# Dynamic convolution with gated projection on one core: softmax loads and stores as single transfers, x loaded by batch from POOL's queue

## The chip, the cores and the metric

The kernel runs on one core of a Trainium2 chip. The metric is the device time of one execution in microseconds. The programs of this case are timed in several runs, and the median counts; one more execution is taken with the hardware profiler, and all rows of the profile come from it.

## What is computed

Two steps on x of shape (8, 4224, 192), in float32. First a dynamic convolution: for each position and each of 8 heads, seven weights go through a softmax and mix the last seven rows of x. Then a gated layer on the result: a causal convolution of five taps per channel gives a gate through a sigmoid, a projection gives a value, and gate times value is projected again.

```python
# attention-like part: B=8, S=4224, D=192, H=8 heads of 24 channels, K=7
w = exp(weight_gen - max(weight_gen, -1)); w = w / (sum(w, -1) + 1e-09)
x_pad = concat(zeros(B, K-1, D), x)                    # causal
a[b,s,h,g] = sum_k w[b,s,h,k] * x_pad[b, s+k, h*24+g]
# gated part, on a
gate_pre[b,s,d] = sum_{k<5} conv_w[k,d] * a_pad[b, s+k, d]
out = (sigmoid(gate_pre) * (a @ w_val)) @ w_out
```

## The kernel before

**Groups.** The sequence is cut into 36 groups of 118 positions (the last has 94), each for all 8 batches. For a group, 128 rows of x (118 and what the convolutions reach back) lie in SBUF as `xt`, partition by row, batch and channel along the free side; three such buffers rotate. The softmax weights of the group lie in `tb` as a banded matrix per batch and head, so that the dynamic convolution becomes matmuls of 128 x 32 by 128 x 122 on TensorE (PE): `bank` (line 432), 128 of them per group in four kinds, one for each pair of half-filled output tiles. Two `tb` buffers rotate.

The row order inside the partitions is special: partition 8 * i + j holds row 16 * j + i of the group. So a chunk j of 16 successive rows sits on every eighth partition, and one transfer fills one chunk for all batches: `load_x` (line 410) and `load_t` (line 419), eight of each per group.

**After the banks.** ScalarE (ACT) copies the results out of PSUM into `A`, `B` and `S` (`evac`, lines 443 to 450). Some heads land apart from the others, in `S`, and eight small transfers per group on POOL's queue (`move`, lines 459 and 461) put them into holes of `A` and `B`. Then the gate's first tap on ACT (line 473), four more on VectorE (DVE, line 478), the sigmoid on ACT (483), the values matmul on PE (`val`, lines 492 to 499), gate times value on DVE (506, 508), the last projection on PE (`omm`, 519 and 526), a copy on ACT (541) and two stores on SP's queue (550).

**Softmax.** It runs ahead of the groups in ten parts. A part of R rows per partition covers 16 R positions of each batch: 128 partitions, partition 8 * q + b for stretch q of batch b. `load` (272) brings the part's weights with a few more rows into `wt`, one transfer per batch, eight in all. Reductions, subtraction, exponential, reciprocal and product follow on DVE and ACT (lines 282 to 307). `spread` (319, ACT) writes the weights, with gaps, into `zt`, twelve rows of a part at a time, and `store` (325) puts these into the DRAM scratch `zd`, again one transfer per batch. `load_t` reads `zd` back as a band. The parts have 8, 8, 16, six times 34, and 28 rows; a part has one to three `zt` pieces, 25 in all.

**The order.** No scheduler sorts the instructions. A planner (`Order`) takes each operation with its engine, an estimated duration, a key and its dependences, plays them through, and issues each engine's instructions in the order so found. The order is fixed in the program: on each engine, and on each engine's DMA queue, an instruction that waits holds up all behind it. The durations given with `add` decide the order, not the time taken on the chip. The queue of a transfer is the engine that issues it: in the program before, SP issues all x and tb loads, all output stores, nearly all softmax loads and a few z stores; POOL issues the moves and most z stores; ACT issues four loads and four stores of the first part.

Of the kernel before, what the change touches and what calls it, by code (L numbers as in the profile page):

```python
# [89 lines left out]
def tile_dynconv_gated_moe(  # L90
# [9 lines left out]
    nc = tc.nc  # L100

    B, S, D = x.shape
    H, K = wg.shape[2], wg.shape[3]
    C = D // H
    KC = conv_w.shape[0]
    P = 128
    HD = P // 2
    Q = 32
    PAD = K - 1
    HALO = KC - 1  # L110
    FRONT = PAD + HALO
# [12 lines left out]
    G = 16  # L124
# [121 lines left out]
    class Softmax:  # L246
# [17 lines left out]

        def load(self, b, eng):
            R, n = self.R, self.n
            flat = self.wt.rearrange("p r h k -> p (r h k)")
            off = wg.offset + (b * S + self.r0) * ROW

            def part(q, c0, c1):  # L270
                src = bass.AP(tensor=wg.tensor, offset=off + c0 * ROW, ap=[[R * ROW, q], [1, (c1 - c0) * ROW]])
                eng.dma_start(out=flat[b:b + B * q - B + 1:B, c0 * ROW:c1 * ROW], in_=src)  # L272

            if b == B - 1 and self.r0 + HP * R == S:
                part(HP, 0, R)
                part(HP - 1, R, n)
            else:
                part(HP, 0, n)

# [40 lines left out]

        def store(self, c, z, b, eng):
            a, e = self.zc[c]
            d0 = zd[b, 1 + self.r0 + a, :]
            dst = bass.AP(tensor=d0.tensor, offset=d0.offset, ap=[[self.R * PITCH, HP], [1, (e - a) * PITCH]])
            eng.dma_start(out=dst, in_=z[b:P:B, 0:e - a].rearrange("p r c -> p (r c)"))  # L325

# [3 lines left out]
    def softmax(r0, R, k0, k1, early, k2, behind=()):  # L330
# [3 lines left out]
        n = s.n * ROW  # L334
        ld = []
        b0 = add("DVE", 0.06, early - 1e-3, s.begin, old, behind=behind)
        for n_, b in enumerate((0, 4, 1, 5, 2, 6, 3, 7)):
            q = QUEUES[n_ % 2] if r0 == 0 else QUEUES[0]
            ld.append(add(q[0], 0.45, early + 1e-3 * n_, lambda b=b, e=q[1]: s.load(b, e), [b0],
                          bytes=HP * n * 4))  # L340
        h = len(s.cut)
# [19 lines left out]
        for c, (a, b) in enumerate(s.zc):  # L361
            z = zt[len(zstore) % 2]
            old = zstore[-2] if len(zstore) > 1 else zinit[len(zstore)]
            need = [nm for nm, (c0, c1) in zip(norms, s.cut) if c0 < b + PAD and c1 > a]
            kk, cp = key(), []
            for e in range(2):
                for o in range(2):
                    cp.append(add("ACT", act((b - a) // 2 * (NPR - o) * H), kk,
                                  lambda c=c, z=z, e=e, o=o: s.spread(c, z, e, o), [*need, *old]))
            sts = []  # L370
            for n_, i in enumerate((0, 4, 1, 5, 2, 6, 3, 7)):
                q = QUEUES[n_ % 2 if r0 == 0 else 0 if len(soft) == 2 else 2]
                sts.append(add(q[0], 0.55, k2, lambda c=c, z=z, i=i, e=q[1]: s.store(c, z, i, e), cp,
                               bytes=HP * (b - a) * PITCH * 4))
            zstore.append(sts)
            last += cp
            rows.append((r0, sts))
# [7 lines left out]
    class Group:  # L385
# [13 lines left out]
        def rows(self, j):  # L399
# [4 lines left out]
            return lo, hi, slice(NGR * lo + j, NGR * (hi - 1) + j + 1, NGR)  # L404

        def load_x(self, j):
            lo, hi, p = self.rows(j)
            src = bass.AP(tensor=x.tensor, offset=x.offset + (self.s - FRONT + G * j + lo) * D,
                          ap=[[D, hi - lo], [S * D, B], [1, D]])
            nc.sync.dma_start(out=self.xb[p, :, 0:D], in_=src)  # L410

# [51 lines left out]
        def part(self, g, j):  # L463

            return (self.B if g else self.A).rearrange("p (b w) -> p b w", w=self.w)[:, :, j:j + self.n]
# [158 lines left out]
    for m, gp in enumerate(gr):  # L624
        if 2 <= m < len(PARTS) - 1:
# [6 lines left out]
        late = (() if m == 0 else T[m - 1]["loadt"]) if m < 3 else ()  # L632
        d["loadx"] = [add("SP", 0.42, (-90, -35, -1)[m] if m < 3 else m - 1.9, lambda gp=gp, j=j: gp.load_x(j), old, bytes=G * B * D * 4, behind=late) for j in gp.chunks]
        use = [o for a, sts in rows if a < gp.s + n for o in sts] + [front]
        old = dep(m - 2, "bank") if m >= 2 else cleared[m % 2]
        d["loadt"] = [add("SP", 0.45, m - 1.8 + 0.01 * j, lambda gp=gp, j=j: gp.load_t(j), [*use, *old],
                          bytes=G * B * RUN * 4) for j in gp.chunks]
# [8 lines left out]
        for q, kind in enumerate((3, 2, 0, 1)):  # L646
# [10 lines left out]
            else:  # L657
# [3 lines left out]
        d["bank"], d["ev"] = list(bank.values()), ev  # L661
        mvB = [add("POOL", 0.6, m + 0.1, lambda gp=gp, k=k, u=u: gp.move(k, u), [*ev[3], *ev[2]], bytes=(Q - C) * HB * w * 4)
               for k in (4, 5) for u in range(2)]
        mvA = [add("POOL", 0.6, m + 0.2, lambda gp=gp, k=k: gp.move(k, 0), [*ev[3], *ev[0], *ev[1]], bytes=(Q - C) * HB * w * 8)
               for k in range(4)]
# [21 lines left out]
        for k in range(2):  # L687
# [3 lines left out]
        d["out"], d["oev"] = o, evs  # L691
        d["store"] = [add("SP", 0.45, m + 2.0, lambda gp=gp, i=i: gp.store(i), evs, delay=4.0,
                          bytes=n * D * 4 * (B if i == 0 else 1)) for i in range(2)]
# [27 lines left out]
```

## Time and profile before

| what | value |
|---|---|
| median of 3 runs | 625.44 us (622.83 to 625.74) |
| the profiled execution's own time | 621.07 us |
| its span, first to last instruction | 619.3 us |
| mean granted TensorE clock | 0.909 |
| busy PE, DVE, ACT, POOL | 490.9, 438.0, 342.3, 259.7 us |
| moved by the DMA engines | 123.20 MB in 135989 packets, mean 199 GB/s |
| x loads, tb loads, SP | 287 and 287 issues |
| softmax loads | 77 issues on SP, 4 on ACT |
| z stores | 176 issues on POOL, 20 on SP, 4 on ACT |
| moves | 288 issues on POOL |

How to read the rows: `L410` is line 410 of the kernel; an engine's name with a q (SPq) is its queue, where DMA issues stand with the time that the issue took, not the transfer. `out<-in` are the program's tile names. In a row of busy time, the number after the comma is the mean of one in ns. A bracket at the end of a row gives the idle time of the engine before it, and what ended it. A granted clock under 1 means that TensorE ran slower in that stretch. Busy PE includes matmuls that wait in its pipeline.

### The profile page before, as it was taken

The numbers are of one execution on the slowest core, as the hardware profiler recorded it, in microseconds if no ns is written. First come the engines' busy times: TensorE is split into PE (matmuls) and PEld (weight loads), VectorE is DVE, ScalarE is ACT, GpSimd is POOL, SyncE is SP. The second block draws the span as 40 slices with busy tenths as digits, with TensorE's granted clock in tenths as the row PEclk, the third lists the DMA queues.
The fourth block names the chain that finished last, engine by engine and source line by source line (L and its number), as shares of the span: only waits on it lengthen the run. The fifth ranks groups of instructions, "written<-read, shape, count | busy, mean of one in ns | idle before, by whom it ended". The sixth has DMA issues, their size and how long they took to land.

```text
span 619.3 us, 16002 instructions
## 1 busy us (share of the span) xinstructions
PE 490.9 (79%) x6278; PEld 335.0 (54%) x6278; DVE 438.0 (71%) x488; ACT 342.3 (55%) x531; POOL 259.7 (42%) x496
## 2 busy tenths in 40 slices
PE   2015289576999598888999997488996899999995
PEld 1012266364658365556666765366665567667753
DVE  5376559676894845987798782987885476867680
ACT  4334365567657434485667854368654546555641
POOL 9155266047434812135550764027634614322220
PEclk7557899979899889997999999589997899999999
DMA  4665579869895976767896799668878777677332
GB/s 121 158 199 156 143 218 283 235 172 270 234 270 150 263 206 169 205 180 193 226 286 180 208 264 253 203 177 245 240 194 255 200 192 183 188 195 192 84 85 85
DMA packets 135989, 123.20 MB, mean 199 GB/s; under 512 B 21866, under 2 KB 130022, under 8 KB 133226
## 3 DMA queue, kind: packets, MB, share of 16 engines
q1 hardware_dynamic: 120026, 90.83, 53.0%
q0 software_dynamic: 15632, 30.76, 17.9%
q8 instruction: 50, 0.82, 0.5%
q10 hardware_dynamic: 256, 0.58, 0.3%
q14 instruction: 25, 0.20, 0.1%
HBM read 64.55 MB, written 51.43 MB: 187 GB/s over the span
## 4 chain that ended last, share of the span: by engine, by line
PE 54%; SPq 24%; DMA 9%; ACT 5%; issue 3%; DVE 2%; POOL 2%; ACTq 0%; DVEq 0%
PE pa L432 16%; PE po L519 13%; SPq L419 10%; PE po L526 7%; SPq L410 7%; PE v L496 7%; SPq L272 5%; PE v L499 4%; PE v L494 4%; PE v L492 4%; DMA tb<-zd 3%; DMA xt<-in_x_dram 2%; DMA zd<-zt 2%; SPq L550 2%; ACT ot L541 1%
## 5 line engine op out<-in xcount | busy, mean ns | idle before, releaser
L432 PE MATMUL pa<-tb,xt 128*32 128x122 f32 (+1 forms) x4608 | 150.7, 290 | 88.4 <-DMA tb<-zd 63.5
L432 PEld LDWEIGHTS pa<-tb,xt 128*32 128x32 f32 x4608 | 138.8, 117 | 104.3 <-issue 88.6
L478 DVE SCALAR_TENSOR_TENSOR aA<-A,wf,aA 128x944 f32<-128x944 f32 (+1 forms) x144 | 171.6, 1191 | 18.6 <-ACT aA L473 13.4
L461 POOL DMA_DIRECT2D B<-S x144 | 74.1, 521 | 250.2 <-ACT B L446 240.8
L478 DVE SCALAR_TENSOR_TENSOR aB<-B,wf,aB 128x472 f32<-128x472 f32 (+1 forms) x144 | 101.2, 703 | 40.1 <-ACT aB L473 30.1
L519 PE MATMUL po<-wf,aA 128*118 128x192 f32 (+1 forms) x576 | 114.9, 344 | 11.4 <-ACT ot L541 6.2
L541 ACT COPY ot<-po 118x768 f32<-118x768 f32 (+1 forms) x72 | 57.7, 802 | 113.2 <-PE po L526 72.5
L519 PEld LDWEIGHTS po<-wf,aA 128*118 128x118 f32 (+1 forms) x576 | 92.6, 185 | 40.6 <-issue 13.8
L325 POOL DMA_DIRECT2D zd<-zt x176 | 85.0, 489 | 49.2 <-ACT zt L319 29.5
L459 POOL DMA_DIRECT2D A<-S x144 | 73.7, 519 | 29.2 <-ACT A L443 22.5
L526 PE MATMUL po<-wf,aB 64*118 64x192 f32 (+1 forms) x576 | 67.3, 352 | 14.7 <-DVE aB L508 10.2
L506 DVE TENSOR_TENSOR aA<-v,aA 128x944 f32<-128x944 f32 (+1 forms) x36 | 40.8, 1135 | 47.4 <-ACT aA L483 34.2
L450 ACT COPY S<-pa 64x488 f32<-64x488 f32 (+1 forms) x72 | 40.4, 561 | 52.1 <-PE pa L432 51.6
L496 PE MATMUL v<-A,wva 128*128 128x472 f32 (+1 forms) x144 | 63.1, 559 | 0.0
L526 PEld LDWEIGHTS po<-wf,aB 64*118 64x118 f32 (+1 forms) x576 | 45.1, 180 | 31.8 <-issue 12.9
L483 ACT ACTIVATE aA<-aA 128x944 f32<-128x944 f32 (+1 forms) x36 | 35.7, 991 | 30.5 <-DVE aA L478 30.5
L443 ACT COPY A<-pa 128x488 f32<-128x488 f32 (+1 forms) x72 | 40.6, 563 | 11.8 <-PE pa L432 10.9
L496 PEld LDWEIGHTS v<-A,wva 128*128 128x128 f32 x144 | 27.4, 190 | 30.5 <-issue 30.0
L492 PE MATMUL v<-A,wvm 128*64 128x472 f32 (+1 forms) x144 | 37.6, 600 | 6.9 <-DMA A<-S 6.9
L319 ACT COPY zt<-wt 128x192 f32<-128x192 f32 (+3 forms) x100 | 39.7, 460 | 4.7 <-DVE wt L307 4.4
L508 DVE TENSOR_TENSOR aB<-v,aB 128x472 f32<-128x472 f32 (+1 forms) x36 | 23.1, 642 | 24.4 <-PE v L494 12.7
L473 ACT ACTIVATE aA<-A,wf 128x944 f32<-128x944 f32 (+1 forms) x36 | 38.9, 1081 | 2.6 <-DMA A<-S 2.6
(59 smaller groups left out, 369.5 us busy)
## 6 DMA issues: line engine op xcount, KB each, us to landing
xt<-in_x_dram SPq DMA_DIRECT2D x285, 96.0 KB
tb<-zd SPq DMA_DIRECT2D x285, 88.0 KB
out_dram<-ot SPq DMA_DIRECT2D x35, 672.0 KB
zd<-zt POOLq DMA_DIRECT2D x112, 138.0 KB, 4.5
wt<-in_weight_gen_dram SPq DMA_DIRECT2D x48, 140.0 KB
zd<-zt POOLq DMA_DIRECT2D x48, 115.0 KB, 4.4
A<-S POOLq DMA_DIRECT2D x140, 30.5 KB, 3.5
B<-S POOLq DMA_DIRECT2D x140, 15.2 KB, 3.1
```

The source lines that it names most:

```text
L325: eng.dma_start(out=dst, in_=z[b:P:B, 0:e - a].rearrange("p r c -> p (r c)"))
L410: nc.sync.dma_start(out=self.xb[p, :, 0:D], in_=src)
L419: nc.sync.dma_start(out=self.t.rearrange("p n a h t -> p n (a h t)")[p, :, c0:c0 + RUN], in_=src)
L432: nc.tensor.matmul(out=pa[Q * c:Q * c + Q, w * j:w * j + w], lhsT=self.xb[:, u * HB + j, C * h:C * h + Q], rhs=self.t[:, u * HB + j, PAD / ...
L459: nc.gpsimd.dma_start(out=self.A[q:q + n], in_=self.S[p:p + n])
L461: nc.gpsimd.dma_start(out=self.B[HD * u + q:HD * u + q + n], in_=self.S[p:p + n, w * u:w * u + w])
L478: nc.vector.scalar_tensor_tensor(out=a, in0=self.part(g, j), scalar=cw[:, g, j:j + 1], in1=a, op0=ALU.mult, op1=ALU.add)
L492: nc.tensor.matmul(out=v2[HD * u:HD * u + HD, 0:n], lhsT=wvm, rhs=A[u], start=True, stop=False, tile_position=(0, HD * u))
L496: nc.tensor.matmul(out=v01[:, u, 0:n], lhsT=wva, rhs=A[u], start=True, stop=False)
L519: nc.tensor.matmul(out=po[0:n, u, D * t:D * t + D], lhsT=self.aA[:, c:c + n], rhs=woa, start=first and t == 0, stop=not first, skip_group_ ...
L526: nc.tensor.matmul(out=po[0:n, u, D * t:D * t + D], lhsT=self.aB[hs, c:c + n], rhs=wob[hs], start=first and t == 0, stop=not first, skip_g ...
L541: nc.scalar.copy(out=self.ot[0:n, :, 2 * k:2 * k + 2, :].rearrange("p u t d -> p u (t d)"), in_=self.po[0:n, :, 0:2 * D])
```

## The change

Transfers that were eight, one per batch or per chunk, are written with different shapes on their two sides.

- A softmax part is loaded by one transfer on SP: 128 successive partitions on the SBUF side, and 16 stretches by 8 batches by a run on the DRAM side. The last part, whose last partition has fewer rows, takes three. 81 issues become 12.
- A `zt` piece is stored by one transfer in the same way: 200 issues become 25. The pieces of the first three parts go on SP, the others on POOL.
- x of groups 1 to 34 is loaded by one transfer per batch, for all 128 partitions: on the DRAM side 16 by 8 by 192 elements with steps of one row and of 16 rows. These 8 per group go on POOL's queue; groups 0 and 35 stay on SP by chunk. The pieces remain rows of 192 elements.
- The planner's durations and keys: x loads 0.55 (were 0.42) and at m - 2.2 (was m - 1.9), tb loads 0.65 (0.45), moves 0.53 (0.6), output stores 0.55 (0.45), softmax loads and z stores 0.6 each.

```diff
--- before.py
+++ after.py
@@ -262,20 +262,21 @@
             if self.r0 + HP * self.R == S:
                 nc.vector.memset(self.wt[P - Q:P, self.R:], 0.0)
 
-        def load(self, b, eng):
+        def load(self, eng):
             R, n = self.R, self.n
             flat = self.wt.rearrange("p r h k -> p (r h k)")
-            off = wg.offset + (b * S + self.r0) * ROW
-
-            def part(q, c0, c1):
-                src = bass.AP(tensor=wg.tensor, offset=off + c0 * ROW, ap=[[R * ROW, q], [1, (c1 - c0) * ROW]])
-                eng.dma_start(out=flat[b:b + B * q - B + 1:B, c0 * ROW:c1 * ROW], in_=src)
-
-            if b == B - 1 and self.r0 + HP * R == S:
-                part(HP, 0, R)
-                part(HP - 1, R, n)
-            else:
-                part(HP, 0, n)
+
+            def part(p, q, nb, c0, c1):
+                src = bass.AP(tensor=wg.tensor, offset=wg.offset + (p % B * S + self.r0 + p // B * R + c0) * ROW,
+                              ap=[[R * ROW, q], [S * ROW, nb], [1, (c1 - c0) * ROW]])
+                eng.dma_start(out=flat[p:p + q * nb, c0 * ROW:c1 * ROW], in_=src)
+
+            if self.r0 + HP * R < S:
+                part(0, HP, B, 0, n)
+            else:
+                part(0, HP - 1, B, 0, n)
+                part(P - B, 1, B - 1, 0, n)
+                part(P - 1, 1, 1, 0, R)
 
         def max(self, k):
             a, b = self.cut[k]
@@ -318,11 +319,12 @@
                           ap=[[z0.ap[0][0], P], [2 * PITCH, n], [CELL, m], [2, H]])
             nc.scalar.copy(out=dst, in_=src)
 
-        def store(self, c, z, b, eng):
+        def store(self, c, z, eng):
             a, e = self.zc[c]
-            d0 = zd[b, 1 + self.r0 + a, :]
-            dst = bass.AP(tensor=d0.tensor, offset=d0.offset, ap=[[self.R * PITCH, HP], [1, (e - a) * PITCH]])
-            eng.dma_start(out=dst, in_=z[b:P:B, 0:e - a].rearrange("p r c -> p (r c)"))
+            d0 = zd[0, 1 + self.r0 + a, :]
+            dst = bass.AP(tensor=d0.tensor, offset=d0.offset,
+                          ap=[[self.R * PITCH, HP], [(1 + S) * PITCH, B], [1, (e - a) * PITCH]])
+            eng.dma_start(out=dst, in_=z[:, 0:e - a].rearrange("p r c -> p (r c)"))
 
     soft = []
     zstore = []
@@ -332,12 +334,8 @@
         s = Softmax(r0, R)
         old = soft[-2]["last"] if len(soft) > 1 else []
         n = s.n * ROW
-        ld = []
         b0 = add("DVE", 0.06, early - 1e-3, s.begin, old, behind=behind)
-        for n_, b in enumerate((0, 4, 1, 5, 2, 6, 3, 7)):
-            q = QUEUES[n_ % 2] if r0 == 0 else QUEUES[0]
-            ld.append(add(q[0], 0.45, early + 1e-3 * n_, lambda b=b, e=q[1]: s.load(b, e), [b0],
-                          bytes=HP * n * 4))
+        ld = [add("SP", 0.6, early, lambda: s.load(nc.sync), [b0], bytes=P * n * 4)]
         h = len(s.cut)
         steps = 5 * h + 1 + len(s.zc)
         done = [0]
@@ -367,11 +365,8 @@
                 for o in range(2):
                     cp.append(add("ACT", act((b - a) // 2 * (NPR - o) * H), kk,
                                   lambda c=c, z=z, e=e, o=o: s.spread(c, z, e, o), [*need, *old]))
-            sts = []
-            for n_, i in enumerate((0, 4, 1, 5, 2, 6, 3, 7)):
-                q = QUEUES[n_ % 2 if r0 == 0 else 0 if len(soft) == 2 else 2]
-                sts.append(add(q[0], 0.55, k2, lambda c=c, z=z, i=i, e=q[1]: s.store(c, z, i, e), cp,
-                               bytes=HP * (b - a) * PITCH * 4))
+            q = QUEUES[0 if len(soft) < 3 else 2]
+            sts = [add(q[0], 0.6, k2, lambda c=c, z=z, e=q[1]: s.store(c, z, e), cp, bytes=P * (b - a) * PITCH * 4)]
             zstore.append(sts)
             last += cp
             rows.append((r0, sts))
@@ -403,11 +398,21 @@
             hi = min(G, self.k - G * j)
             return lo, hi, slice(NGR * lo + j, NGR * (hi - 1) + j + 1, NGR)
 
+        def whole(self):
+            return 0 < self.m < NM - 1
+
         def load_x(self, j):
-            lo, hi, p = self.rows(j)
-            src = bass.AP(tensor=x.tensor, offset=x.offset + (self.s - FRONT + G * j + lo) * D,
-                          ap=[[D, hi - lo], [S * D, B], [1, D]])
-            nc.sync.dma_start(out=self.xb[p, :, 0:D], in_=src)
+
+            r0 = self.s - FRONT
+            if self.whole():
+                src = bass.AP(tensor=x.tensor, offset=x.offset + (j * S + r0) * D,
+                              ap=[[D, G], [G * D, NGR], [1, D]])
+                nc.gpsimd.dma_start(out=self.xb[:, j, 0:D], in_=src)
+            else:
+                lo, hi, p = self.rows(j)
+                src = bass.AP(tensor=x.tensor, offset=x.offset + (r0 + G * j + lo) * D,
+                              ap=[[D, hi - lo], [S * D, B], [1, D]])
+                nc.sync.dma_start(out=self.xb[p, :, 0:D], in_=src)
 
         def load_t(self, j):
             lo, hi, p = self.rows(j)
@@ -630,10 +635,12 @@
 
         old = T[m - 3]["bank"] if m >= 3 else [*xpad, xz]
         late = (() if m == 0 else T[m - 1]["loadt"]) if m < 3 else ()
-        d["loadx"] = [add("SP", 0.42, (-90, -35, -1)[m] if m < 3 else m - 1.9, lambda gp=gp, j=j: gp.load_x(j), old, bytes=G * B * D * 4, behind=late) for j in gp.chunks]
+        d["loadx"] = [add("POOL" if gp.whole() else "SP", 0.55, (-90, -35, -1)[m] if m < 3 else m - 2.2,
+                          lambda gp=gp, j=j: gp.load_x(j), old, bytes=G * B * D * 4, behind=late)
+                      for j in (range(B) if gp.whole() else gp.chunks)]
         use = [o for a, sts in rows if a < gp.s + n for o in sts] + [front]
         old = dep(m - 2, "bank") if m >= 2 else cleared[m % 2]
-        d["loadt"] = [add("SP", 0.45, m - 1.8 + 0.01 * j, lambda gp=gp, j=j: gp.load_t(j), [*use, *old],
+        d["loadt"] = [add("SP", 0.65, m - 1.8 + 0.01 * j, lambda gp=gp, j=j: gp.load_t(j), [*use, *old],
                           bytes=G * B * RUN * 4) for j in gp.chunks]
         def lent(name):
 
@@ -659,9 +666,9 @@
                 e1 = add("ACT", act(HB * w, True), m - 0.5, lambda gp=gp, kind=kind: gp.evac(kind, 1), [b, e0])
                 ev[kind] = [e0, e1]
         d["bank"], d["ev"] = list(bank.values()), ev
-        mvB = [add("POOL", 0.6, m + 0.1, lambda gp=gp, k=k, u=u: gp.move(k, u), [*ev[3], *ev[2]], bytes=(Q - C) * HB * w * 4)
+        mvB = [add("POOL", 0.53, m + 0.1, lambda gp=gp, k=k, u=u: gp.move(k, u), [*ev[3], *ev[2]], bytes=(Q - C) * HB * w * 4)
                for k in (4, 5) for u in range(2)]
-        mvA = [add("POOL", 0.6, m + 0.2, lambda gp=gp, k=k: gp.move(k, 0), [*ev[3], *ev[0], *ev[1]], bytes=(Q - C) * HB * w * 8)
+        mvA = [add("POOL", 0.53, m + 0.2, lambda gp=gp, k=k: gp.move(k, 0), [*ev[3], *ev[0], *ev[1]], bytes=(Q - C) * HB * w * 8)
                for k in range(4)]
         d["moves"] = mvA + mvB
 
@@ -689,7 +696,7 @@
                          [*gv, conv["o"], *(evs[-1:] if k else dep(m - 1, "oev")[-1:])], mode=(("64r", "128"), ("128", "64r"))[k]))
             evs.append(add("ACT", act(4 * D, True), m + 1.2, lambda gp=gp, k=k: gp.oev(k), [o[-1], *(lent("store") if k == 0 else [])]))
         d["out"], d["oev"] = o, evs
-        d["store"] = [add("SP", 0.45, m + 2.0, lambda gp=gp, i=i: gp.store(i), evs, delay=4.0,
+        d["store"] = [add("SP", 0.55, m + 2.0, lambda gp=gp, i=i: gp.store(i), evs, delay=4.0,
                           bytes=n * D * 4 * (B if i == 0 else 1)) for i in range(2)]
     od.run()
 
```

## The prediction

> **What bounds the kernel now.** I read the page first, then the busy times by stage, then the SP queue in order of time, because nobody on the page looks full: PE, the busiest engine, is at 79%.
>
> ```profile
> span 619.3 us, 16002 instructions
> ...
> PE 490.9 (79%) x6278; PEld 335.0 (54%) x6278; DVE 438.0 (71%) x488; ACT 342.3 (55%) x531; POOL 259.7 (42%) x496
> ...
> q1 hardware_dynamic: 120026, 90.83, 53.0%
> q0 software_dynamic: 15632, 30.76, 17.9%
> ```
>
> The last two rows are the DMA queues: packets, MB, and packet time as a share of 16 engines' span. Together 70.9%. So no engine and no transfer path is full on average; the limit must change by stage. The busy times of five stages (us per engine, granted clock, DMA share, GB/s):
>
> ```profile
> 0.00:77.00 77.00, 19.88 (x284) 12.46 (x284) 46.55 (x64) 30.71 (x52) 39.64 (x56) 0.69 0.57 155
> 77.00:300.00 223.00, 185.22 (x2524) 129.42 (x2526) 159.98 (x171) 131.44 (x201) 96.52 (x194) 0.93 0.78 219
> 300.00:345.00 45.00, 43.71 (x443) 27.76 (x443) 40.95 (x46) 30.60 (x45) 19.27 (x39) 1.00 0.81 228
> 345.00:500.00 155.00, 132.18 (x1710) 92.27 (x1704) 109.78 (x121) 88.86 (x144) 74.64 (x151) 0.90 0.80 223
> 500.00:600.00 100.00, 98.22 (x1262) 65.43 (x1261) 75.96 (x84) 56.71 (x85) 29.59 (x58) 1.00 0.61 159
> ```
>
> The columns after the length are PE, PEld, DVE, ACT, POOL. From 500 on PE is 98% busy: it is the bound there. From 77 to 500 PE idles 37.8 + 1.3 + 22.8 = 61.9 us. What ends that idle time, in the chain of waits of PE between 77 and 612:
>
> ```profile
> PE pa L432 <- DMA tb<-zd: 22.2, 6, 9.7
> PE pa L432 <- DMA xt<-in_x_dram: 21.3, 4, 8.0
> ```
>
> 43.5 of the 61.9 us end with a transfer that SP issues. Are these late because the wires are full, or because SP gets to them late? The SP queue in order of time (start, length, line, count):
>
> ```profile
> 184.17 10.91 SPq L419 DMA_DIRECT2D tb<-zd  x7
> ...
> 227.05 6.08 SPq L419 DMA_DIRECT2D tb<-zd  x8
> 233.18 5.10 SPq L410 DMA_DIRECT2D xt<-in_x_dram  x8
> 238.38 4.97 SPq L272 DMA_DIRECT2D wt<-in_weight_gen_dram  x8
> 243.45 5.37 SPq L410 DMA_DIRECT2D xt<-in_x_dram  x7
> ```
>
> Each row starts where the one above it ended (227.05 + 6.08 = 233.13, and so on). SP never rests; tb of a group stands in line behind x and softmax loads that are needed later. That is the first half of the answer. The second half is the row at 184.17: seven issues took 10.91 us, 1.56 us each, where eight took 4.97 us at 238.38. SP's issue itself gets longer when transfers in front of it are slow. So SP is the bound in the middle, partly by its count of issues and partly by the transfers.
>
> **What it costs per issue, and the floor.** Minimum, median and maximum ns of one issue:
>
> ```profile
> L410 SPq DMA_DIRECT2D xt<-in_x_dram x287: 553/599/2607, 3.7 to 564.8; - x144
> L419 SPq DMA_DIRECT2D tb<-zd x287: 532/599/2854, 36.3 to 571.4; - x144
> L272 SPq DMA_DIRECT2D wt<-in_weight_gen_dram x77: 492/587/1071, 0.7 to 391.5; - x77
> L325 SPq DMA_DIRECT2D zd<-zt x20: 498/587/731, 20.5 to 60.9; - x20
> L550 SPq DMA_DIRECT2D out_dram<-ot x72: 318/534/1859, 105.1 to 614.7; - x72
> ```
>
> At medians SP has 287 x 0.599 + 287 x 0.599 + 77 x 0.587 + 20 x 0.587 + 72 x 0.534 = 439 us of issuing. PE's floor comes from three successive starts of a whole group's bank matmuls in the PE-bound tail, 12.88 and 12.82 us apart, of which the first and last are shown:
>
> ```profile
> 77.23 5.16 PE L432 MATMUL pa<-tb,xt 128*32 128x122 f32 x128 [8.05 <-DMA xt<-in_x_dram]
> ...
> 546.84 3.77 PE L432 MATMUL pa<-tb,xt 128*32 128x122 f32 x128
> ...
> 572.54 3.77 PE L432 MATMUL pa<-tb,xt 128*32 128x122 f32 x128
> ```
>
> 25.70 / 2 = 12.85 us per group. PE's 361.1 busy us from 77 to 500 are then about 28.1 groups, which took 423 us: 15.05 us per group. The same 128 matmuls take 5.16 us after a wait and 3.77 us in a full stretch, so a removed wait gives back more than itself.
>
> **The change part by part.**
>
> Softmax loads: 77 issues on SP (and four on ACT) become 12, all on SP. Rows per partition and bytes stay. A single issue for 128 partitions isn't in the trace as a softmax load; bounded by the tb row (128 pieces, 0.599) and by the longest out issue (1.859). I take 0.6: the tb issue has the same number of pieces. Cost on SP: -65 x 0.6 = -39 us.
>
> z stores: 176 on POOL, 20 on SP and 4 on ACT become 21 on POOL and 4 on SP (the one of the second part moves from POOL to SP). SP: -16 x 0.587 = -9 us. The ACT queue loses four issues and nothing waits for it there: nothing gained.
>
> x by batch: the 34 whole groups' 272 issues leave SP for POOL. SP: -272 x 0.599 = -163 us. SP keeps 15 + 287 + 12 + 4 + 72 = 390 issues, 439 - 39 - 9 - 163 = 228 us; per whole group 8 x 0.599 + 2 x 0.534 = 5.9 us against PE's 12.85. SP is no bound any more, and tb stands behind nothing but out stores.
>
> POOL takes them. Rows for it:
>
> ```profile
> L325 POOL DMA_DIRECT2D zd<-zt x176: 484/484/682, 31.5 to 495.8; - x176
> ...
> L461 POOL DMA_DIRECT2D B<-S x144: 512/518/634, 48.1 to 589.7; - x144
> ...
> L200 POOL DMA_DIRECT2D ot<-wd x3: 617/626/627, 15.4 to 17.9; - x3
> ```
>
> An x issue on POOL has 128 rows. Lower bound 0.484 (a store of 16 rows), upper 1.56 (the stretched SP row). I take 0.626, the weight load, since it too fills up to 128 partitions. POOL: -155 x 0.484 + 272 x 0.626 = -75 + 170 = +95 us, so 259.7 becomes 355. Per group: 8 moves x 0.518 + 8 x 0.626 + 0.6 store x 0.5 = 9.5 us of 12.85. It holds, with 3 us of air. What stands behind an x load on POOL is the moves into A and B; the taps on ACT and DVE wait for these. An x load waits for the bank of three groups earlier, which ends just before the moves of that same group become ready, so it should rarely stop a move that could go. If it does, a move is late by up to 8 x 0.626 = 5 us, and the values matmul of that group is one whole group (12.85 us) further on in PE's order: covered, unless DVE is full. The new planning figures (0.53, 0.55, 0.65) are nearer to the rows (0.518, 0.626, 0.599) than the old 0.42 and 0.6; I cost the reordering at nothing, as DVE (71%) and ACT (55%) have air; without it, the idle that now waits on them stays.
>
> The start, 0 to 77. DVE idles for the second part's load and SP is again continuous:
>
> ```profile
> 10.93 9.43 SPq L272 DMA_DIRECT2D wt<-in_weight_gen_dram  x8
> ...
> 31.26 4.96 SPq L272 DMA_DIRECT2D wt<-in_weight_gen_dram  x8
> 36.33 5.23 SPq L419 DMA_DIRECT2D tb<-zd  x8
> ...
> 50.97 10.49 SPq L325 DMA_DIRECT2D zd<-zt  x16
> ...
> 63.43 6.28 SPq L410 DMA_DIRECT2D xt<-in_x_dram  x8
> ```
> ```profile
> 23.56 0.97 DVE L282 TENSOR_REDUCE mx<-wt 128x112 f32<-128x784 f32 x1 [11.14 <-DMA wt<-in_weight_gen_dram]
> ```
>
> Before the third bank starts at 77.23, SP drops 24 softmax loads, 16 z stores and 16 x loads: 56 issues at about 0.64 with the gap, 36 us. Upper bound 36 (all of it on the path), lower bound 11.1 (DVE's wait alone, while DVE's and ACT's own chains then set the pace). I take 20: DVE is busy 46.55 of 77, so squeezing out more than some 25 would leave it no slack. A loss here is possible too: the x loads of groups 1 and 2 now go through POOL, which converts weights at that time, 2 x 8 x 0.626 = 10 us; they fit into POOL's 77 - 39.64 us of air, so I count nothing.
>
> The middle, 77 to 500. The bytes stay, and so does the packets' time: (223 x 0.78 + 45 x 0.81 + 155 x 0.80) = 334 us at a full path. How full can it run? Three dense stretches:
>
> ```profile
> 140.00:160.00 20.00, 15.99 (x286) 11.94 (x286) 13.86 (x16) 15.13 (x20) 13.26 (x28) 0.91 0.88 259
> 160.00:180.00 20.00, 18.54 (x98) 10.56 (x92) 18.20 (x21) 12.68 (x21) 10.88 (x23) 1.00 0.93 270
> ...
> 300.00:320.00 20.00, 20.00 (x180) 12.24 (x178) 18.52 (x22) 13.68 (x24) 12.41 (x26) 1.00 0.86 246
> ```
>
> At 0.86 it takes 388 us (35 gained), at 0.93 359 us (64 gained, the same as all of PE's idle). I take the middle row, 0.88: 334 / 0.88 = 380, so 43 us gained. The third row shows PE with no idle at a share of 0.86, so PE at its floor and the transfers near theirs are compatible. After 500 nothing changes: SP isn't the bound there.
>
> Sum, against the profiled execution: 619.3 - 20 - 43 = 556.3 span; its own time was 621.07, 1.8 over its span: 558. The median of the runs, 625.44, is 0.7% above 621.07, so I forecast 562.
>
> **The rivals.**
>
> (A) The transfer path takes SP's place. For it: 1.56 us per SP issue at 184, and shares up to 0.93. Then two queues only push harder on something full, and the middle keeps nearly its share of 0.80: 334 / 0.80 = 418, 5 us gained, and the start gains its lower 11: 619.3 - 16 + 1.8 = 605, 609 in terms of the median. A halfway case, 0.84, gives 398, 25 gained: about 586 with 15 at the start. Against it: the third dense row. The Trainium skill, "DMA: Bandwidth & Descriptors", section "Issuing engines are not separate DMA queues", speaks for this rival: transfers started from several engines run on the same 16 DMA engines, and spreading them saves the sequencer's issue time only. By that rule alone the 211 us that SP no longer issues are the whole gain to be had, and none of it where the path was full; the trace agrees at 184 and not at 238, where an issue took 0.62 us.
>
> (B) POOL becomes the bound: slower than before. POOL's queue waits on its own earlier transfers:
>
> ```profile
> 376.52 0.53 POOL L461 DMA_DIRECT2D B<-S  x1 [0.75 <-DMA zd<-zt]
> ```
> ```profile
> DMA to landing us min/median/max: 2.3/4.4/8.3
> ```
>
> The first row is a move that waits for a z store which it doesn't read; counted back, it is the transfer eight issues earlier, so I take it (an inference) that eight can be under way. The second is the landing of z stores. With 16.6 issues per group POOL then needs 16.6 x L / 8 per group: 9.1 us at the median 4.4, no wait; above L = 6.2 it passes PE's 12.85; above 7.6 it costs more than the present 15.05 plus the start's gain (20 / 28.1 = 0.7). At 8.3 it is 17.2 us, 28.1 x (17.2 - 15.05) = +60 in the middle, 20 back at the start: 661, 666 in terms of the median. Against it: 4.4 stands for stores whose eight parts came in one burst, the worst neighbours that queue had.
>
> (C) SP's relief uncovers the order: DVE waits for late moves, and the middle gains little although SP and the path have air. A move late by 5 us in every second of 28.1 groups, with DVE unable to catch up, costs 70 us against 63 gained: 619.3 + 7, within 0.5% to 1% of before. Against it: xt has three buffers, the load goes 2.2 groups ahead.
>
> (D) Better than forecast: all 61.9 us of idle and 25 at the start: 532 + 1.8, 538 in terms of the median.
>
> **How the numbers follow.** Forecast (545 to 577) 0.50; D 0.12; A 0.26, most of it at the halfway 586 and the less at 609; C 0.04; B 0.08. 0.5% is 3 us, about what this measurement tells from no change. Faster 0.88, same 0.04, slower 0.08. Range: from D, with some of the start's upper bound, 528, to most of A, 604; B and C stay outside, with the ends of A and D.
>
> **What would show it.** Right: SP's rows with gaps between them in the middle; PE's waits on tb and xt under 15 us together; the third bank before 62; DMA share 0.86 or more between 80 and 440; POOL's x issues near 0.63. Wrong: x issues on POOL over 1.1 us or POOL waiting on x transfers (B); tb issues still stretched over 1 us with a share of 0.8 (A); DVE idle before L478 on moves (C).

## The result, and the profile after

The changed kernel takes 589.45 us (median of 4 runs, 587.95 to 591.1) against 625.23 us before (4 runs): ratio 0.9436, 95% interval 0.9396 to 0.9475. The forecast was 562, in a range of 528 to 604. The direction holds; the gain is 36 us where 63 were forecast. Where a run of one of the kernels below was disturbed (one took 2601 us), its ratio leaves that run out and its median doesn't. The profiled execution took 587.95 us. From its page, the span, the engines and the two DMA queues (packets, MB, packet time as a share of 16 engines' span):

```profile
span 586.2 us, 15839 instructions
...
PE 484.9 (83%) x6278; PEld 327.0 (56%) x6278; DVE 438.5 (75%) x488; ACT 345.0 (59%) x533; POOL 330.2 (56%) x613
...
q1 hardware_dynamic: 79779, 65.40, 42.5%
q0 software_dynamic: 26016, 56.75, 36.1%
```

The span lost 33.1 us. The next two views of the changed kernel show where: busy times by stage (PE, PEld, DVE, ACT, POOL, then granted clock, DMA share, GB/s), and PE's matmuls in order of time.

```profile
0.00:77.00 77.00, 26.95 (x508) 20.15 (x508) 49.14 (x65) 35.61 (x62) 52.53 (x82) 0.71 0.81 199
77.00:300.00 223.00, 187.39 (x2348) 125.93 (x2348) 175.55 (x191) 140.23 (x212) 125.15 (x240) 0.94 0.86 231
300.00:345.00 45.00, 45.00 (x539) 29.82 (x538) 38.61 (x41) 29.25 (x46) 26.38 (x51) 0.95 0.86 232
345.00:500.00 155.00, 147.93 (x1934) 98.95 (x1934) 122.74 (x136) 98.40 (x153) 101.33 (x195) 0.99 0.85 228
```
```profile
38.71 5.18 PE L437 MATMUL pa<-tb,xt 128*32 128x122 f32 x128 [33.57 <-DMA tb<-zd]
52.69 5.11 PE L437 MATMUL pa<-tb,xt 128*32 128x122 f32 x128 [8.80 <-DMA tb<-zd]
61.44 1.01 PE L497 MATMUL v<-A,wvm 128*64 128x472 f32 x4 [3.64 <-DMA A<-S]
...
67.65 6.44 PE L437 MATMUL pa<-tb,xt 128*32 128x122 f32 x224
```

- **Start.** The third group's bank began at 77.23 and begins at 67.65: 9.6 us gained. The split hangs on this mark, which is the forecast's: by the first, second and fourth group's bank (43.61, 65.50 and 93.48 before; 38.71, 52.69 and 71.23 after) it would be 4.9, 12.8 and 22.3 us.
- **After it.** From the third bank to the end of the span 542.1 us became 518.5: 23.6 gained. Between 77 and 500, PE idles 35.6 + 0 + 7.1 = 42.7 us instead of 61.9.

What ends PE's idle time from 77 to 500, and SP's (line waited before, releaser, us in total, times, longest):

```profile
PE po L531 <- ACT ot L546: 15.0, 4, 7.8
PE po L531 <- DVE aB L513: 9.9, 3, 5.7
PE po L524 <- DVE aA L511: 9.4, 7, 2.9
...
PE pa L437 <- DMA tb<-zd: 0.7, 1, 0.7
```
```profile
SPq L424 <- PE pa L437: 99.8, 21, 10.0
```

The 43.5 us in which PE waited for x and tb are 0.7, as the forecast's mechanism has it, and SP, which hardly rested, now waits about 100 us for banks to free the tb buffer. But PE has new waits, on the chain behind the banks (value, gate, output copy). The rest of the text is about these. The chain of work that ended last leads back through one of them, from PE's 6.42 us of idle time at 109.43:

```profile
76.93 11.81 DMA zd<-zt
88.74 0.28 issue
89.02 6.28 DMA A<-S
...
95.40 1.09 ACT aA L478
...
109.43 1.64 PE po L531 x8
```

POOL's queue in order of time, at the same place:

```profile
76.39 1.08 POOL L327 DMA_DIRECT2D zd<-zt  x2 [0.42 <-DMA xt<-in_x_dram]
77.49 2.08 POOL L466 DMA_DIRECT2D B<-S  x4
79.56 1.03 POOL L464 DMA_DIRECT2D A<-S  x2
83.59 0.52 POOL L464 DMA_DIRECT2D A<-S  x1 [3.00 <-DMA zd<-zt]
89.02 0.52 POOL L464 DMA_DIRECT2D A<-S  x1 [4.91 <-DMA zd<-zt]
```

Two z stores go out, then four and two moves: eight issues. The ninth, at 83.59, waits for the first of them, and the tenth, at 89.02, for the second, which landed at 76.93 + 11.81 = 88.74. Neither move reads what a z store writes. So the forecast's inference that eight can be under way holds here, and a slow 1.1 MB store stops two small moves that ACT's first tap (95.40) waits for. The trace's records also show what asks for this wait. POOL's 594 transfers report their landing on eight semaphores (counters that an instruction can wait for), taken in turn, and the move at 83.59 waits, before it is issued, for the semaphore that the store at 76.39 raises. It is a wait that stands in the program; no run here shows that the queue itself holds no more than eight.

From 77 to 500, what POOL waits for in the changed kernel, and in the kernel before (one row: the largest wait there that a transfer ends):

```profile
POOL A L464 <- DMA zd<-zt: 36.9, 12, 7.4
POOL A L464 <- DMA B<-S: 11.9, 3, 5.0
POOL A L464 <- DMA xt<-in_x_dram: 10.3, 7, 3.7
```
```profile
POOL zd L325 <- DMA zd<-zt: 10.6, 13, 2.0
```

All POOL waits that a transfer ends come to 13 us before and 84 us after. And the transfers take longer to land. Landing of POOL's transfers, count, KB each and median us, in the changed kernel:

```profile
zd<-zt POOLq DMA_DIRECT2D x14, 1104.0 KB, 8.1
A<-S POOLq DMA_DIRECT2D x140, 30.5 KB, 4.4
B<-S POOLq DMA_DIRECT2D x140, 15.2 KB, 4.8
```

Before, these were 4.5 us for a z store of 138 KB, 3.5 and 3.1.

### The profile page after: what moved, and what is told of

Same layout as the page of the kernel before. It is cut to its first block, busy times and chain, and to the rows that moved or that the text cites. A ratio compares the mean times of both kernels' runs of the same rounds, so it can differ in the third digit from the quotient of the medians.

```text
span 586.2 us, 15839 instructions
## 1 busy us (share of the span) xinstructions
PE 484.9 (83%) x6278; PEld 327.0 (56%) x6278; DVE 438.5 (75%) x488; ACT 345.0 (59%) x533; POOL 330.2 (56%) x613
## 4 chain that ended last, share of the span: by engine, by line
PE 40%; DMA 30%; POOL 13%; issue 8%; ACT 4%; DVE 2%; SPq 1%; POOLq 0%; ACTq 0%; DVEq 0%
DMA zd<-zt 13%; PE po L524 10%; PE pa L437 10%; POOL xt L410 7%; DMA A<-S 6%; PE po L531 5%; DMA xt<-in_x_dram 5%; PE v L501 5%; DMA tb<-zd 3%; PE v L499 3%; PE v L504 3%; PE v L497 3%; POOL A L464 2%; DMA raw_c<-cd 1%; POOL B L466 1%
## 5 line engine op out<-in xcount | busy, mean ns | idle before, releaser
L437 PE MATMUL pa<-tb,xt 128*32 128x122 f32 (+1 forms) x4608 | 140.5, 276 | 48.8 <-DMA tb<-zd 43.1
L410 POOL DMA_DIRECT2D xt<-in_x_dram x272 | 143.8, 549 | 44.0 <-DMA A<-S 8.7
L437 PEld LDWEIGHTS pa<-tb,xt 128*32 128x32 f32 x4608 | 127.7, 110 | 64.0 <-issue 56.1
L524 PE MATMUL po<-wf,aA 128*118 128x192 f32 (+1 forms) x576 | 117.2, 349 | 11.8 <-DVE aA L511 9.4
L524 PEld LDWEIGHTS po<-wf,aA 128*118 128x118 f32 (+1 forms) x576 | 94.6, 188 | 43.2 <-issue 20.1
L464 POOL DMA_DIRECT2D A<-S x144 | 74.2, 521 | 69.2 <-DMA zd<-zt 36.9
L531 PE MATMUL po<-wf,aB 64*118 64x192 f32 (+1 forms) x576 | 68.6, 358 | 26.6 <-ACT ot L546 16.8
L499 PE MATMUL v<-B,wvd 128*128 128x472 f32 (+1 forms) x72 | 39.3, 627 | 0.0
```

Of the source, the lines that this page charges most:

```text
L410: nc.gpsimd.dma_start(out=self.xb[:, j, 0:D], in_=src)
L437: nc.tensor.matmul(out=pa[Q * c:Q * c + Q, w * j:w * j + w], lhsT=self.xb[:, u * HB + j, C * h:C * h + Q], rhs=self.t[:, u * HB + j, PAD / ...
L464: nc.gpsimd.dma_start(out=self.A[q:q + n], in_=self.S[p:p + n])
L499: nc.tensor.matmul(out=v2[:, 0:n], lhsT=wvd, rhs=Bt, start=False, stop=True)
L524: nc.tensor.matmul(out=po[0:n, u, D * t:D * t + D], lhsT=self.aA[:, c:c + n], rhs=woa, start=first and t == 0, stop=not first, skip_group_ ...
L531: nc.tensor.matmul(out=po[0:n, u, D * t:D * t + D], lhsT=self.aB[hs, c:c + n], rhs=wob[hs], start=first and t == 0, stop=not first, skip_g ...
```

## The experiments

Theories, as the expectations number them. (1) POOL's queue: the moves stand behind x loads and large z stores, so the chain behind the banks is late. (2) The transfer path is the limit. (3) VectorE is. (4) At the start, one softmax load of 1.1 MB delays what the first groups need. (5) The written order and the start set the rest, wherever the waits appear.

**The softmax half alone.** x stays by chunk on SP, with planning figures 0.65 and m - 1.9.

```diff
         def whole(self):
-            return 0 < self.m < NM - 1
+            return False
```

> Only the softmax loads and z stores as single transfers; x by chunk on SP as before. SP has 390 us of issuing at medians instead of 439, POOL loses 75 us and gets nothing. Theory 1: POOL's moves stand behind a z store only with eight issues between, SP is near its limit again: 595 to 608 us. Theory 2: same bytes, a queue less busy: 588 to 595 us.

Measured: 625.65 us, ratio 1.0023 (0.9983 to 1.0063). No gain at all, outside every expectation. SP in order of time:

```profile
238.64 5.22 SPq L415 DMA_DIRECT2D xt<-in_x_dram  x3
243.96 4.79 SPq L555 DMA_DIRECT2D out_dram<-ot  x2
248.79 4.57 SPq L415 DMA_DIRECT2D xt<-in_x_dram  x5
```

Though about 80 issues are gone, SP is still full: two output stores took 2.04 and 2.70 us each, with no wait in or before them. From 77 to 500 SP waited 38 us and issued 468 transfers, (423 - 38) / 468 = 0.82 us each; before it waited 18 us and issued 535, 0.76 each. The issues that remain are longer and wait more; why they lengthen isn't shown. The third group's bank starts at 65.88, 11 us sooner than before, but that is lost again: PE still waits for x and tb between 77 and 500,

```profile
PE pa L437 <- DMA xt<-in_x_dram: 16.8, 2, 10.1
...
PE pa L437 <- DMA tb<-zd: 10.3, 3, 4.8
```

and of the 39 + 9 us that the forecast takes off SP here nothing reaches the end.

**x alone.** Softmax loads and z stores remain eight each; x goes by batch to POOL, with the changed planning figures.

```diff
-        d["loadx"] = [add("SP", 0.42, ... m - 1.9, ... for j in gp.chunks]
+        d["loadx"] = [add("POOL" if gp.whole() else "SP", 0.55, ... m - 2.2, ...
+                      for j in (range(B) if gp.whole() else gp.chunks)]
```

> Only x by batch on POOL; softmax loads and z stores in eights as before. POOL has 259.7 + 149 = 409 us of issuing, 21 issues per group. Theory 1: the pieces of a z store land sooner (4.4 us) but eight of them fill all places of POOL's queue, so moves still wait: 590 to 605 us. Theory 2: 586 to 592 us.

Measured: 621.57 us, ratio 0.9978 (0.9933 to 1.0023), outside both expectations. Its page, and PE's waits from 77 to 500:

```profile
PE 488.2 (79%) x6278; PEld 326.1 (53%) x6278; DVE 435.0 (71%) x488; ACT 343.5 (56%) x533; POOL 406.2 (66%) x768
```
```profile
PE v L502 <- DMA A<-S: 31.4, 8, 7.6
```

SP is free here and PE no longer waits for x or tb, but it waits 31.4 us for moves, which POOL, 406 us busy and with x loads in front of them, brings late. As these two runs read, the halves need each other. x off SP frees SP; the coalesced softmax takes 155 issues off POOL, which makes the room for x. Alone, each gives nothing that can be told from zero; together 5.6%.

**Is the path the limit?** Four of the eight batches are stored; the others' output is left out.

```diff
-                          ap=[[D, hi - lo], [S * D, B], [1, D]])
-            nc.sync.dma_start(out=dst, in_=self.ot[lo:hi].rearrange("p u t d -> p (u t) d"))
+                          ap=[[D, hi - lo], [S * D, HB], [1, D]])
+            nc.sync.dma_start(out=dst, in_=self.ot[lo:hi, 0].rearrange("p t d -> p t d"))
```

> The changed kernel storing only four of the eight batches of each group's output: 13 MB of 123 MB fewer, the same number of issues. Theory 2: the packets' time of 461 us falls by about 48, and the middle shortens by 25 to 40, so 550 to 565 us. Theory 1: the z stores land somewhat earlier, no more, so 578 to 588 us.

Measured: 592.82 us, ratio 0.9505 (0.9433 to 0.9577), above both expectations. Busy times of its middle:

```profile
77.00:300.00 223.00, 191.72 (x2355) 129.07 (x2356) 177.21 (x193) 140.90 (x213) 126.69 (x242) 0.93 0.81 213
```

The share falls from 0.86 to 0.81, the time doesn't. Theory 2 falls, as far as output bytes can show it.

**Is VectorE?** The maximum and its subtraction are left out of the softmax; the exponential then waits for the load itself.

```diff
-            m = (s.cut[k][1] - s.cut[k][0])
-            a = add("DVE", dve(m * ROW), key(), lambda k=k: s.max(k), ld)
-            subs.append(add("DVE", dve(m * ROW), key(), lambda k=k: s.sub(k), [a]))
-        ex = add("ACT", ..., key(), s.exp, subs)
+            key(), key()
+        ex = add("ACT", ..., key(), s.exp, ld)
```

> The changed kernel without the softmax's maximum and its subtraction: 43 us less work for VectorE, the same transfers. Theory 3: PE's waits that end with VectorE or ACT shrink, 555 to 575 us. Theory 1: POOL's moves wait as before for the z stores, 580 to 590 us.

Measured: 591.63 us, ratio 0.9472 (0.9411 to 0.9532), near theory 1's 580 to 590.

```profile
PE 493.9 (83%) x6278; PEld 333.2 (56%) x6278; DVE 400.2 (68%) x452; ACT 344.8 (58%) x533; POOL 328.6 (56%) x613
```

DVE does 38 us less, and nothing comes of it: theory 3 falls, as far as this part of DVE's work can show it.

**The z stores off POOL.** All 25 on SP.

```diff
-            q = QUEUES[0 if len(soft) < 3 else 2]
+            q = QUEUES[0]
```

> Theory 1 (POOL's queue): a POOL issue waits for the landing of the one eight issues earlier, and a z store of 1.1 MB lands only after 8.1 us (median), so the moves behind it wait (36.9 us in 12 waits), and with them the taps, the gate and PE. With the z stores on SP's queue these waits go: 15 to 25 of the 42.7 us that PE idles between 77 and 500 go too, so 565 to 575 us. Theory 2 (the transfer path is full, share 0.86 between 77 and 500): the bytes stay, so 586 to 592 us, and the moves wait for something else.

Measured: 583.47 us, ratio 0.9341 (0.9259 to 0.9423), between the two expectations; in a second set, on one chip with the changed kernel again:

> The changed kernel with all z stores on SP's queue, beside the changed kernel: theory 1 says 5 to 10 us less than that, since 36.9 us of waits on POOL go and others, on x loads, take a part of their place; theory 5 says the same within 3 us.

> The changed kernel once more, on the same chip as the next two: 586 to 592 us by every theory.

587.94 us, 0.9423 (0.9372 to 0.9474), against 589.13 us, 0.9464 (0.9418 to 0.9511), for the changed kernel. These two can't be told apart: theory 1's 5 to 10 us are missed, and theory 5's 3 us fit. So the place of the z stores is worth about 1% at the most, though it takes away POOL's largest wait for a transfer. POOL's waits in the first set, from 77 to 500, offer a reason:

```profile
POOL B L466 <- DMA xt<-in_x_dram: 43.0, 17, 5.1
...
POOL A L464 <- DMA xt<-in_x_dram: 19.8, 11, 3.7
```

What the moves don't wait for z stores, they wait for x loads: 63 us (41 in the second set) where the changed kernel has 15.

**Half of x back on SP,** with the z stores there too.

```diff
-                nc.gpsimd.dma_start(out=self.xb[:, j, 0:D], in_=src)
+                (nc.gpsimd if j % 2 else nc.sync).dma_start(out=self.xb[:, j, 0:D], in_=src)
```

The planner's queue for x changes with it.

> The z stores on SP as in the run before, and x of the whole groups half on SP (even batches), half on POOL. Theory 1 (a queue's issue waits for the landing of the one eight issues earlier; POOL's moves stand behind x): with 12 instead of 16 issues per group on POOL, the 63 us that moves waited for x loads in the run before fall under 25, and 583.5 becomes 568 to 577 us. Theory 3 (VectorE's chain paces the middle: 88% busy between 77 and 300 in the run before): the waits go and the time stays, 580 to 587 us.

Measured: 589.76 us, ratio 0.9463 (0.9426 to 0.95): theory 1's 568 to 577 is missed. The moves' waits went as it had it. From 77 to 500 they wait 3.7 + 2.9 + 1.3 = 7.9 us for transfers, where the changed kernel's wait 36.9 + 11.9 + 10.3 + 4.4 = 63.5:

```profile
POOL A L464 <- DMA xt<-in_x_dram: 3.7, 2, 2.4
```

The time didn't follow. In the whole run PE waits for x on SP,

```profile
PE pa L437 <- DMA xt<-in_x_dram: 42.2, 3, 32.1
```

but nearly all of that comes before the first two banks, where the changed kernel waits 33.57 + 8.80 us for tb, and these banks start no later (37.54 and 52.44, after 38.71 and 52.69). So this isn't where the gain went. From 77 to 500 PE idles 40.2 us, close to the changed kernel's 42.7. Either the moves' waits behind other transfers cost little, or half of x on SP costs as much elsewhere; this run doesn't tell which.

**x issued behind the moves,** with the z stores on SP. The x loads of group m are put in the order behind the moves of group m - 3.

```diff
-        late = (() if m == 0 else T[m - 1]["loadt"]) if m < 3 else ()
+        late = (() if m == 0 else T[m - 1]["loadt"]) if m < 3 else T[m - 3]["moves"]
```

> The z stores on SP, and x of group m put behind the moves of group m - 3 in POOL's order. Theory 1: an x load rarely stands right in front of a move, the 63 us of waits on x loads shrink to under 30: 568 to 578 us. If the x loads simply take longer to land than the time between two groups' moves allows, the waits stay: 580 to 587 us.

Measured: 582.46 us, ratio 0.9346 (0.9296 to 0.9396), on the same chip as the 589.13 of the changed kernel: 1.1% better, and the intervals don't touch. It is the best version found, but what theory 1 expected is missed. Against the z stores on SP alone, in the same set, 0.9423 (0.9372 to 0.9474), the intervals overlap, so the order's own part isn't shown. POOL's waits from 77 to 500:

```profile
POOL B L466 <- DMA xt<-in_x_dram: 29.9, 13, 5.3
...
POOL A L464 <- DMA xt<-in_x_dram: 17.8, 13, 3.4
```

The moves wait 48 us for x, not under 30, and no less than the 41 of z_sp in the same set: with eight x loads and eight moves per group in one queue, this order doesn't get them out of each other's way.

**The moves on SP.**

```diff
-        mvB = [add("POOL", 0.53, m + 0.1, ...
+        mvB = [add("SP", 0.58, m + 0.1, ...
```

The same for `mvA`, and `nc.gpsimd` becomes `nc.sync` in `move`.

> The changed kernel with the 288 moves on SP's queue; POOL keeps x and the z stores. Theory 1: no move stands behind a z store any more, 36.9 us of POOL's waits go: 568 to 580 us. Against it: on SP the moves stand behind tb loads that wait for PE's banks (111 us of waits on SP): 590 to 620 us if that order decides.

Measured: 637.96 us, ratio 1.0228 (1.0186 to 1.0271): slower than before the change, and than either expectation. The largest of PE's waits from 77 to 500:

```profile
PE pa L437 <- ACT S L455: 28.3, 7, 10.5
```

A moved queue isn't only a count of issues: SP's order, tb loads and output stores with waits of their own, now holds up the moves, and POOL, with x and z stores alone, waits 295 us for banks in the whole run. This is read from the waits; nothing else was tried with it.

**No moves.** The values that lie in `S` never reach `A` and `B`; what is computed from these is not the reference's.

```diff
-        mvB = [add("POOL", 0.53, m + 0.1, ...
-        mvA = [add("POOL", 0.53, m + 0.2, ...
+        mvA = mvB = []
```

> The changed kernel without the 288 moves: the taps and the values matmuls read A and B as ACT wrote them, so this part of the result is left out; all other work and transfers stay. Theory 1 (what is left of the idle time comes from moves that are late in POOL's queue): nothing waits there for a z store or an x load any more except x itself, most of the 42.7 us of PE's idle between 77 and 500 goes and some of the start's, 540 to 562 us. Theory 5 (the written order and the start set the rest, wherever the waits appear): 575 to 588 us.

Measured: 548.14 us, ratio 0.8771 (0.8706 to 0.8836), as theory 1 had it.

```profile
77.00:300.00 223.00, 214.54 (x2885) 145.96 (x2887) 192.77 (x209) 152.49 (x231) 72.47 (x138) 0.98 0.81 230
```

PE idles 8.5 us from 77 to 300 where the changed kernel idles 35.6. What hangs on the moves is worth 589.13 - 548.14 = 41 us of the changed kernel. This is an upper bound for POOL's waits: the edit takes away 149 us of POOL's issuing (288 x 0.518) and the step from copy over landing to tap as well. So it shows that the time hangs on the moves, not that it hangs on their waits.

**The start.** The fourth part's 1.1 MB load is put behind the tb loads of the second group.

```diff
-    ... -69, at - 1.7, rows[0][1])
+    ... -69, at - 1.7, T[1]["loadt"])
```

> The changed kernel with the 1.1 MB softmax load of the fourth part, issued at 21.3 us in front of the last half of group 0's tb loads, put behind group 1's tb loads. Theory 4 (the start is held by transfers that stand behind large ones): the first bank starts near 30 instead of 38.7 us, and the whole takes 580 to 586 us. Otherwise, the chain of the converted weights sets the start: 586 to 592 us.

Measured: 594.17 us, ratio 0.9512 (0.9462 to 0.9562): no gain. The profiled execution is longer than the others (span 599.1), so only its start is read: the first bank starts at 33.32 instead of 38.71, and then PE waits (0 to 77)

```profile
PE v L497 <- DMA A<-S: 12.7, 1, 12.7
```

for a move. Theory 4 is right in that the load delays the first bank, wrong in that this sets the start: the third bank begins at 65.21 instead of 67.65.

## Why the forecast was right in sign and too large

**SP as the bound: right.** The forecast's reading that SP hardly rests (18 us of waits from 77 to 500), and that PE's waits on x and tb go once it does, is what the trace shows (43.5 to 0.7 us). What it left out is the next in line: x_only has SP free and gains nothing. Relief of SP was not sufficient; that it was necessary is argued from soft_only, where SP stayed full and nothing was gained.

**"SP's issue itself gets longer", read at 184.17: wrong row.** The forecast divided 10.91 us by seven issues. The same stretch of the kernel before, in a smaller window, with SP's rows and its waits:

```profile
193.26 1.82 SPq L419 DMA_DIRECT2D tb<-zd  x3
```
```profile
SPq L419 <- PE pa L432: 6.1, 1, 6.1
```

The timeline joins instructions of one line over a wait; 6.1 of the 10.91 us were SP waiting for a bank, and the issues themselves took 532 to 880 ns, median 598. The upper bound of 1.56 us for an x issue, and half of what spoke for rival A, with its "the trace agrees at 184", rested on a wait taken for an issue. That issues do stretch is true nonetheless (0.76 us each with a median of 0.599, and the two output stores of soft_only); so 228 us of SP work after the change was too low, but SP has 187 us of waits to spare from 77 to 500, and nothing hangs on it.

**x on POOL at 0.626: close, on the high side.**

```profile
L410 POOL DMA_DIRECT2D xt<-in_x_dram x272: 518/548/634, 18.4 to 512.2; - x136
```

272 x 0.548 = 149 us instead of 170, and POOL is busy 330 us, not 355.

**"It should rarely stop a move", and if so "covered": the step that fell short.** The forecast considered what an x load waits for (the bank three groups earlier), and not what a move waits for once eight other issues are under way before it. POOL's waits that a transfer ends went from 13 to 84 us. "Covered" was argued from the values matmul alone, and for that it held: PE's wait for moves there is 1.5 us from 77 to 500. It left out the gate, which hangs on the moves too. PE now waits on its far end, the product of gate and value and the output copy: 15.0 + 9.9 + 9.4 + 1.5 = 35.8 of 42.7 us. The chain shown above leads from one of these waits back to a move; the others weren't followed. That the moves matter, no_moves shows (41 us). That it is by their waits in POOL's queue isn't shown, and z_sp_x_split, with nearly all of these gone and the same time, speaks against it. Rivals B and C pointed at this place; B's price was far too high because it gave every transfer the landing of a z store. Only 21 of POOL's issues are such stores. x loads land after 4.2 us, moves after 4.4 and 4.8, below the 6.2 us at which B would begin.

**z landing of 4.4: not the new store's.** The term came from stores of 138 KB. One store of eight times the bytes lands after 8.1 us, up to 11.8. As a whole it isn't slower: in the trace of before, the 14 full bursts of eight took 9.6 us at the median from the first issue to the last landing, waits between the issues included.

**The middle, 43 us: mis-sized, 23.6 measured.** The share rose to the forecast's level (0.86 from 80 to 440), but the packet time didn't stay. By the page it was 0.709 x 619.3 = 439 us and is 0.786 x 586.2 = 461 us, for nearly the same bytes (121.6 and 122.2 MB on these two queues). And half_out, with a share of 0.81, is as slow: output bytes didn't set the time. That 589 lies beside rival A's halfway 586 is a coincidence of numbers.

**The start, 20 us: mis-sized, 9.6 measured, below its lower bound of 11.1.** The forecast's sign, a third bank before 62, is missed. That bound was DVE's wait for one load. DVE's waits from 0 to 77 after the change:

```profile
DVE wf L221 <- POOL wf L220: 11.1, 2, 9.6
...
DVE mx L283 <- DMA wt<-in_weight_gen_dram: 4.6, 3, 2.1
```

The wait for loads fell by 6.5 us, and a wait for POOL's weight conversion rose by 7.1 (before: 4.0). The forecast gave the x loads of the first groups POOL's air at no price; POOL's rows of the changed kernel have it otherwise:

```profile
58.23 0.54 POOL L410 DMA_DIRECT2D xt<-in_x_dram  x1 [3.73 <-DMA tb<-zd]
...
68.64 1.03 POOL L220 TENSOR_TENSOR wf<-wf,aA 128x384 f32<-128x384 f32 x1
```

The conversion that ended at 58.35 before ends at 69.67, behind x loads and moves that wait. But the third bank starts at 67.65, before that end, so this isn't what set it: it follows the values matmuls without a gap, and these waited 3.64 us for a move (61.44 above), behind a second bank that waited 8.80 us for tb. The late conversion can only have cost time after the mark. This is read from the trace; no run took it apart.

**Rival D** fell with the moves: even with none, 548.

**Open.** The sum of POOL's waits on transfers doesn't rank the kernels (29 us in z_sp_x_split, 49 in x_only, which gained nothing, 84 in the changed kernel, 94 in z_sp), so that sum isn't the price; which of these waits count, if any, no run isolated. How the 41 us divide between waits behind transfers under way, longer landings, and the bare length of the chain from copy to tap is open, and so is how much the kernel before would gain without its moves, which wasn't run. The reordering, costed at nothing, wasn't tried by itself.

## What to carry to other kernels

When issues move from a full queue to another, ask what small, urgent transfer stands behind them there: by the program's own waits it can be held until an earlier transfer has landed, and a sum of issue times doesn't show that. Then follow everything that hangs on it, the gate here as well as the values matmul. But a wait that is long on an engine isn't yet a price: nearly all of the moves' waits went in one run, and the time stayed. Two queues near their limit may have to be relieved together; each half of this change alone gave nothing. And divide a stretch of a queue's timeline by its count only after looking for waits inside it.

## What the runs showed of the hardware that was not expected

- POOL's ninth transfer waits for the landing of the first, whatever the two touch: at 83.59 and 89.02 above, and at 309.22, where a move waits 7.42 us for the z store issued eight before it at 297.63. The trace's eight semaphores, taken in turn, show this as a wait of the program. Whether the hardware would take a ninth isn't shown.
- One 1.1 MB store lands after 8.1 us at the median, each of eight of 138 KB after 4.5, but their burst as a whole after 9.6. With x on POOL and z in eights (x_only) the moves land after 3.6 and 2.9 us; with z in one piece too, after 4.4 and 4.8.
- The Trainium skill, "DMA: Bandwidth & Descriptors", section "Issuing engines are not separate DMA queues", says that starting transfers from several engines saves issue time alone. x_only saved SP that time and gained nothing (0.9978). In moves_sp the same 288 transfers on another queue cost 8% (ratios 1.0228 and 0.9436 to the kernel before).
